# Layer 1's softmax numerators go to scratch memory, and the freed buffers keep K and V blocks

## The chip, the cores and the metric

One Trainium2 chip, one core. The metric is device time in microseconds from start to end of one launch. Each kernel is run several times, and the median is given.

## What is computed

Four layers in a row, with one token: attention, feed-forward, attention, feed-forward, and then the gradient of all of it. Both attention layers use the same cached K and V (4 heads of 65,536 keys, 128 wide, bfloat16; 67 MB each), and 32 query heads, 8 to each K/V head. Both feed-forward layers share their weights too.

```
x = x + A(layernorm(x))     # A: q = x@wq, softmax(q k^T / sqrt(128)) v, @wo
x = x + B(layernorm(x))     # B: relu(x@w1 + b1)^2 @ w2 + b2
x = x + A(layernorm(x))
x = x + B(layernorm(x))
out, vjp = jax.vjp(forward, ...); return (out, *vjp(grad_out))
```

The outputs are the result and the gradients of x, K, V, wq, wo, w1, b1, w2 and b2. The gradients of K and V are as large as K and V, and each is the sum over the two attention layers.

## The kernel before

K and V do not fit on the chip, so they are streamed four times. The passes are numbered 0 to 3. Pass 0 (`attn_fwd`, named L1) is the first attention layer forward, pass 1 (`attn_fwd`, L3) the second one forward, pass 2 (`attn_bwd3`) the second one's backward for the query gradient, and pass 3 (`attn_bwd4`) does the first one's backward together with the gradients of K and V for both layers, and writes them. Between passes lie the dense parts (wo, w1, w2, wq), with nothing of K and V to do.

**Blocks.** On-chip memory for streaming is one `ARENA`, cut into 20 blocks of 128 partitions x 4096 bfloat16, 1 MB each (1.0486e6 bytes). Everything large takes such a block: 32 keys x 128 partitions of K or of V (a head has 16 blocks), a piece of a weight, a tile of gradients waiting to be stored, or a numerator plane. `take_one` and `take_pair` hand out free blocks, oldest first as a rule, when the program is built; a load then waits on the chip until the last user of its block is done. `HELD` blocks are not handed out. Loads are issued by the SP queue in program order, and most are 2 MB (two neighbouring blocks). Stores are issued by the POOL queue.

**Numerator planes.** A pass over a head computes scores, and ACT writes exp(score - running maximum) as bfloat16 into the head's plane (`E`, one block for each layer and head). Pass 2 reads the planes of layer 3, pass 3 those of both layers. So 8 of the 20 blocks (`NSLOT` = 12 are left) end up held from the forward passes to pass 3, where `E_done` frees both planes of a head as it is finished.

**Kept blocks.** Consecutive passes run through the heads and keys in opposite directions, so the last blocks of one pass are the first of the next. `NKEEP = [8, 7, 7]` blocks stay on the chip between passes 0 and 1 (K), 1 and 2 (V), 2 and 3 (V), and are not loaded again. Kept K in pass 0 and kept V in pass 2 are stored transposed (`turned_to`). In pass 1, V is used untransposed, so kept V blocks are turned by an added transpose in `v8` (`early_turn`, L1117 in the profile), all but those of the last three loads of the pass.

**A step** is 1024 keys: 8 tiles of 128. In pass 0 and 1, stage `kT` transposes 8 K tiles on PE and copies them out of PSUM (L164 on DVE, L161 on ACT), `kS` makes the scores two steps later, and `v8` multiplies numerators and V 36 steps after `kT` (`FWD_LAG`). A head is 64 steps, a pass 256. In pass 2, `vT`, `vS` and `k8` do the same with V first. Passes 0 to 2 have their PE, DVE and ACT order as written; in pass 3 a scheduler orders the instructions.

**Pass 3** has for each block: `vT` and `vS` (dP by PE into the one score buffer `ps_dp`), DVE's product of dP and the numerators of both layers into `X` (L1370), POOL's copy of the numerators of both layers side by side into `xin` (L1330, one buffer), PE transposes of `xin` and `X` (L1336), gradient products on PE (L1393) whose results ACT and DVE convert into a block, and a 1 MB store from POOL (L1399). `k8` (L1424) is the query gradient. The V side runs up to 16 steps ahead of the rest at the start. The weight gradients are made in the background and stored from POOL too.

Of the kernel before, what the change touches and what calls it, by code (L numbers as in the profile page):

```python
# [10 lines left out]
BF = mybir.dt.bfloat16  # L11
# [5 lines left out]
P = 128  # L17
# [3 lines left out]
def kernel(  # L21
# [44 lines left out]
    TLEAD = 2  # L66
    STORE_STEPS = 5
    WAIT_STEPS = 5
    NSLOT = 12
    NWT = 6  # L70
    NKEEP = [8, 7, 7]
    NRING = 5

    const = ctx.enter_context(tc.tile_pool(name="const", bufs=1))
# [179 lines left out]

    BLK = J * DH
    JW = 2 * J
    NG = NSLOT + 2 * G
    assert C * R == BLK
    ARENA = slotp.tile([P, NG * BLK], BF, name="arena")
    GRAN = [ARENA[:, i * BLK:(i + 1) * BLK] for i in range(NG)]  # L260
# [4 lines left out]
    def wide(i):  # L265
        return ARENA[:, i * BLK:(i + 2) * BLK]

    def plane(lay, g):
        return NSLOT + G * lay + g

    def hold(i):
        HELD.add(i)
# [544 lines left out]
    def after(n, fn):  # L817
        TASKS.setdefault(NOW["i"] + n, []).append(fn)
# [52 lines left out]
        return L  # L871


    EALL = ARENA[:, NSLOT * BLK:].rearrange("p (l g c r) -> p l g c r", l=2, g=G, r=R)

    def E(lay, g, c0, n):
        assert plane(lay, g) in HELD and plane(lay, g) not in BUSY
        return EALL[:, lay, g, c0:c0 + n, :]

    def E2(g, c0, n):  # L880
        return EALL[:, :, g, c0:c0 + n, :].rearrange("p l c r -> p c l r")

    def E_done(g, c0, n):

# [5 lines left out]
    def split2(t):  # L890
        return t.rearrange("p c (l r) -> p c l r", l=2)


    def gsl(g):
        return slice(g * R, (g + 1) * R)
# [89 lines left out]
    def attn_fwd(p, L, on_group, bg, end=()):  # L985
# [56 lines left out]
        def stats(g, su, S, pm):  # L1042
            first = su == first_su[g]
            nm = L["negm"][:, g, su, :]
            v = {}

            def lows():
                pmn = tmp.tile([P, R], F32, name="pmn")
                if SU > HB:
                    pmx = tmp.tile([P, R], F32, name="pmx")  # L1050
                    nc.vector.tensor_reduce(out=pmx[:], in_=pm[:, :, :], axis=AX.X, op=ALU.max)
                    pin = pmx[:]
                else:
                    pin = pm[:, :, 0]
                if first:
                    nc.vector.tensor_scalar(out=pmn[:], in0=pin, scalar1=-SCALE, scalar2=None, op0=ALU.mult)
                else:
                    nc.vector.scalar_tensor_tensor(out=pmn[:], in0=pin, scalar=-SCALE, in1=L["negm"][:, g, prev_su[(g, su)], :],
                                                   op0=ALU.mult, op1=ALU.min)
                v["pmn"] = pmn  # L1060

            def turn():
                v["ptm"] = ps_mv([R, P], F32)
                nc.tensor.transpose(v["ptm"][:, :], v["pmn"][:, :], ident_f[:, :])

            def low():
                gm = tmp.tile([R, 1], F32, name="gm")
                nc.vector.tensor_reduce(out=gm[:], in_=v["ptm"][:], axis=AX.X, op=ALU.min)
                v["gmb"] = tmp.tile([R, P], F32, name="gmb", bufs=1)
                nc.vector.tensor_scalar(out=v["gmb"][:], in0=ones_f[0:R, :], scalar1=gm[:, 0:1], scalar2=None, op0=ALU.mult)  # L1070

            def spread():
                v["pnb"] = ps_mv([P, R], F32)
                nc.tensor.matmul(v["pnb"][:, :], lhsT=v["gmb"][:, :], rhs=ident_f[0:R, 0:R], start=True, stop=True)

            def exps():
                nc.vector.tensor_copy(out=nm, in_=v["pnb"][:])  # L1077
                if not first:
                    df = tmp.tile([P, R], F32, name="df")
                    nc.vector.tensor_tensor(out=df[:], in0=nm, in1=L["negm"][:, g, prev_su[(g, su)], :], op=ALU.subtract)  # L1080
                    al = spool.tile([P, R], F32, name="al", tag="al", bufs=3)
                    nc.scalar.activation(out=al[:], in_=df[:], func=ACTF.Exp)
                    state[("al", g, su)] = al
                v["rs"] = spool.tile([P, R], F32, name="rs", tag="rs", bufs=3)
                state[("rs", g, su)] = v["rs"]
                add_load(act=R * 0.5, dve=1.2)

            def exp2(h0):
                def f():
                    c0 = su * SU  # L1090
                    for h in (h0, h0 + 1):
                        nc.scalar.activation(out=E(p, g, c0, SU)[:, :, h], in_=S[:, h, :], func=ACTF.Exp,  # L1092
                                             bias=L["negm"][:, g, su, h:h + 1], scale=SCALE, accum_out=v["rs"][:, h:h + 1])
                return f
            for n, fn in ((1, lows), (3, turn), (4, low), (6, spread), (7, exps), (7, exp2(0)), (8, exp2(2)), (9, exp2(4)), (10, exp2(6))):
                after(n, fn)

        def v8(g, c8):
            su = c8 // SU
# [45 lines left out]
        def group_out(g, su, on):  # L1145
            nc.vector.reciprocal(out=L["rZ"][:, gsl(g)], in_=state["pz"][:])
            nc.vector.tensor_tensor(out=L["oT"][:, gsl(g)], in0=on[:], in1=L["rZ"][:, gsl(g)], op=ALU.mult)
            nc.vector.tensor_copy(out=L["oTb"][:, gsl(g)], in_=L["oT"][:, gsl(g)])
            on_group(g)
            fd = tmp.tile([P, NSU, R], F32, name="fd")  # L1150
            nc.vector.tensor_tensor(out=fd[:], in0=L["negm"][:, g, su, :].unsqueeze(1).to_broadcast([P, NSU, R]),
                                    in1=L["negm"][:, g, :, :], op=ALU.subtract)
            nc.scalar.activation(out=L["fw"][:, g, :, :], in_=fd[:], func=ACTF.Exp)
# [2 lines left out]
        early_turn = set(k for k in TOUCH[p][:-3] if k in KV["keep"])  # L1156
        n = len(items) // G
        order = list(dict.fromkeys(g for g, _ in items))
        holds = [(k * n + 2, plane(p, g)) for k, g in enumerate(order) if k > 0]
        if p == 0:  # L1160
            holds.append((len(items) - 40, plane(1, ITEMS[1][0][0])))
        with tc.manual_schedule(engines=ORDERED):
            pipeline(items, [(kT, 0), (kS, TLEAD), (v8, FWD_LAG)], bg, end, holds)
        st.close()
# [100 lines left out]
    def attn_bwd4(p, La, Lb, on_group, bg, stack, end=()):  # L1265
# [5 lines left out]
        state = {}  # L1271
        gfirst = {g: next(c8 for gg, c8 in items if gg == g) for g in range(G)}
        glast = {g: [c8 for gg, c8 in items if gg == g][-1] for g in range(G)}
        sufirst, sulast = {}, {}
        for g, c8 in items:
            sufirst.setdefault((g, c8 // SU), c8)
# [50 lines left out]
        def eIn(g, c8):  # L1327
            if c8 % J == 0:
                xin = dspool.tile([P, J, R2], BF, name="xin", tag="xin", bufs=1)
                nc.gpsimd.tensor_copy(out=split2(xin[:, :, :]), in_=E2(g, c8, J))  # L1330
                state["xin"] = xin

        def x_transpose(src):
            pt = ps_tr()
# [6 lines left out]
        def vS(g, c8):  # L1341
            if c8 == gfirst[g]:
                g_setup(g)
            vt = state.pop(("vt", g, c8))
            for i in range(8):
                s = (c8 + i) % J
                if s == 0:
                    state["ps_dp"] = ps_sc([P, J, R2])
                    nc.tensor.matmul(state["ps_dp"][:, :, :].rearrange("p c r -> p (c r)"), lhsT=sel2[:, :],
                                     rhs=state["ndt"][:, :].unsqueeze(1).to_broadcast([64, J, R2]), start=True, stop=False)  # L1350
                w = min(4, J - s)
                nc.tensor.matmul(state["ps_dp"][:, s:s + w, :].rearrange("p a b -> p (a b)"), lhsT=vt[:, i, :],  # L1352
                                 rhs=DOB[:, g, 0:w, :].rearrange("p a b -> p (a b)"), start=False, stop=(s == J - 1))
            if is_turned("v", g, c8):
                kv_done("v", g, c8)
                if c8 % J == J - 8 and nexts:
                    NOW["newest"] = True
                    kv8(*nexts.popleft())
                    NOW["newest"] = False
                    NOW["ring"] = not nexts  # L1360
            if (c8 + 8) % J == 0:
                c0 = c8 + 8 - J
                ps_dp = state["ps_dp"]
                if g == items[0][0]:
                    if c8 == J - 8 + items[0][1]:
                        state["Xs"] = Slot("xs")
                    X = state["Xs"].t.rearrange("p (n j r) -> p n j r", j=J, r=R2)[:, c0 // J % 8, :, :]
                else:
                    X = dspool.tile([P, J, R2], BF, name="X", tag="X", bufs=3)
                nc.vector.tensor_tensor(out=split2(X[:, :, :]), in0=split2(ps_dp[:, :, :]), in1=E2(g, c0, J), op=ALU.mult)  # L1370
                add_load(dve=0.13 + J * R2 * 0.00105)
                state[("X", g, c0 // J)] = X

# [59 lines left out]
                    on_group(g)  # L1433

        start_pass(p)
        for b in range(2):
            kv8("k", *items[b * J // 8])
        RING.update(sorted(FREE)[:2])
# [139 lines left out]
        yield from g_mv(w2_slabs()[0], FC, DC, lambda kc: L["gb"][:, kc:kc + 1], ps, fin, side=side)  # L1578


    hold(plane(0, ITEMS[0][0][0]))
    L1["n"], L1["nb"], L1["rstd"] = ln_fwd(x0, "L1")
    run(g_q(L1, 0, ps_mv))
    nc.vector.tensor_copy(out=x1[:], in_=x0[:])
# [290 lines left out]
```

## Time and profile before

| | |
|---|---|
| median of 3 runs | 1956.67 us (1956.1 to 1964.63) |
| the profiled execution: time | 1959.29 us |
| the profiled execution: span | 1957.5 us |
| PE, DVE, ACT, POOL busy | 82%, 60%, 53%, 7% |
| mean granted TensorE clock | 0.912 |
| moved by the transfers | 787.65 MB, mean 402 GB/s |

The span runs from the first to the last instruction of one execution. PE is the matrix engine, PEld its weight loads, DVE the vector engine, ACT the scalar engine, POOL GpSimd, SP the engine that issues loads. The slices cut the span into 40 equal parts of 48.9 us. Rows of groups read: line, engine, operation, tile written <- tile read, shapes, count, then busy time in us and the mean of one in ns, then the idle time before them and what ended it. PE's busy time overlaps weight loads and is not a measure of its peak. By the trace pass 0 runs to about 350 us, pass 1 from about 400 to 745, pass 2 from about 785 to 1140, pass 3 from about 1180 to the end.

### The profile page before, as it was taken

Reading aid. Unit: us, or ns where it says so; the run is one execution under the profiler, and the core shown is the slowest. Engines: PE = TensorE matmul, PEld = TensorE weight load, DVE = VectorE, ACT = ScalarE, POOL = GpSimd, SP = SyncE. Lnnn points to the kernel's source line nnn. Section 1 sums busy time; section 2 is a strip of 40 time slices with the busy share of each in tenths; the row PEclk is TensorE's granted clock in tenths of the full one; section 3 lists DMA queues with packets and bytes.
Section 4 is the critical chain, followed back from the end, with each engine's and each line's share of the span. In section 5 each row is a group of like instructions: output and inputs, shape, how many; then the busy total and the mean of one; then the engine's idle time right before and its main releaser. Section 6 shows DMA issues by size and latency. Waiting matters only on the chain. (4 is left out here: it accounts for less than half of the span.)

```text
span 1957.5 us, 67228 instructions
## 1 busy us (share of the span) xinstructions
PE 1609.0 (82%) x30319; PEld 1313.9 (67%) x30319; DVE 1169.7 (60%) x2421; ACT 1039.4 (53%) x1600; POOL 142.1 (7%) x321
## 2 busy tenths in 40 slices
PE   6878788687878878878787888887888898789897
PEld 6878778687877778777776885554555465455554
DVE  5655455255545544535454576766777686767666
ACT  3444334254334444436363455766777686667666
POOL 0000000000000000000000001111111111111211
PEclk9999999699999999999899998888897898788978
DMA  9999999999999999899999987999999999999996
GB/s 395 426 427 427 426 427 410 400 400 425 428 426 427 428 412 315 328 425 428 426 423 420 403 319 283 415 425 403 384 424 424 426 424 411 370 424 424 424 405 259
DMA packets 106015, 787.65 MB, mean 402 GB/s; under 512 B 9329, under 2 KB 16511, under 8 KB 42111
## 3 DMA queue, kind: packets, MB, share of 16 engines
q1 hardware_dynamic: 81646, 617.65, 76.7%
q0 software_dynamic: 24080, 165.70, 20.3%
q8 instruction: 237, 3.88, 0.7%
q14 instruction: 52, 0.42, 0.1%
HBM read 617.62 MB, written 165.69 MB: 400 GB/s over the span
## 5 line engine op out<-in xcount | busy, mean ns | idle before, releaser
L164 DVE COPY kt<-ps_tr 128x1024 bf16<-128x1024 bf16 x724 | 496.5, 688 | 423.8 <-PE ps_tr L1009 243.7
L161 ACT CAST arena<-ps_gg 128x1024 bf16<-128x1024 f32 x457 | 445.9, 1012 | 224.7 <-PE ps_gg L1393 140.7
L1009 PE MATMUL ps_tr<-ident_b,arena 128*128 128x128 bf16 x3840 | 307.9, 225 | 40.2 <-DMA arena<-in_A_k_cache_dram 29.7
L164 DVE CAST arena<-ps_gg 128x1024 bf16<-128x1024 f32 (+2 forms) x186 | 222.3, 1195 | 112.4 <-PE ps_gg L1471 46.9
L161 ACT COPY kt<-ps_tr 128x1024 bf16<-128x1024 bf16 x164 | 171.1, 1049 | 191.9 <-PE ps_tr L1201 114.9
L1009 PEld LDWEIGHTS <-arena 128*128 128x128 bf16 x3840 | 232.8, 101 | 48.9 <-DMA arena<-in_A_k_cache_dram 32.7
L1111 PE MATMUL ps_acc<-arena 128*128 128x64 bf16 (+4 forms) x4096 | 205.9, 196 | 59.8 <-DMA arena<-in_A_v_cache_dram 50.0
L1393 PE MATMUL ps_gg<-GG,xt 64*128 64x512 bf16 x1024 | 218.2, 423 | 27.3 <-DVE arena L164 10.8
L1111 PEld LDWEIGHTS <-arena 128*128 128x128 bf16 x4096 | 159.6, 100 | 65.8 <-DMA arena<-in_A_v_cache_dram 54.4
L1092 ACT ACTIVATE arena<-S_sb,L_negm 128x128 bf16<-128x128 f32 x256 | 165.6, 1003 | 58.4 <-DVE L_negm L1077 48.6
L1027 PE MATMUL ps_sc<-L_qpad,kt 128*128 128x64 bf16 (+7 forms) x3584 | 182.3, 194 | 15.6 <-ACT kt L161 7.4
L1201 PE MATMUL ps_tr<-ident_b,arena 128*128 128x128 bf16 x1920 | 155.3, 226 | 43.9 <-DMA arena<-in_A_v_cache_dram 40.5
L1321 PE MATMUL ps_tr<-ident_b,arena 128*128 128x128 bf16 x1824 | 181.9, 236 | 6.5 <-DMA arena<-in_A_v_cache_dram 3.8
L1027 PEld LDWEIGHTS <-kt 128*128 128x128 bf16 x3584 | 152.3, 100 | 19.4 <-ACT kt L161 9.8
L1321 PEld LDWEIGHTS <-arena 128*128 128x128 bf16 x1824 | 119.9, 105 | 63.6 <-issue 57.2
L1201 PEld LDWEIGHTS <-arena 128*128 128x128 bf16 x1920 | 117.5, 101 | 47.2 <-DMA arena<-in_A_v_cache_dram 42.1
L1424 PEld LDWEIGHTS <-arena 128*128 128x128 bf16 x2048 | 95.7, 103 | 60.3 <-issue 42.7
L1092 ACT ACTIVATION_READ_ACCUMULATOR arena<-S_sb,L_negm 128x1 f32 x256 | 127.9, 500 | 0.0
L1352 PEld LDWEIGHTS <-kt 128*128 128x128 bf16 x1824 | 85.1, 103 | 50.6 <-issue 49.2
L1352 PE MATMUL ps_sc<-DOB,kt 128*128 128x64 bf16 (+3 forms) x1824 | 115.0, 200 | 0.0
L1424 PE MATMUL ps_acc<-X,arena 128*128 128x64 bf16 (+3 forms) x1536 | 102.1, 200 | 12.5 <-DMA arena<-in_A_k_cache_dram 12.5
L1393 PEld LDWEIGHTS <-xt 64*128 64x128 bf16 x1024 | 64.3, 94 | 71.5 <-issue 34.1
(306 smaller groups left out, 2183.2 us busy)
## 6 DMA issues: line engine op xcount, KB each, us to landing
arena<-in_A_k_cache_dram SPq DMA_DIRECT2D x86, 2048.0 KB, 20.7
arena<-in_A_v_cache_dram SPq DMA_DIRECT2D x83, 2048.0 KB, 21.0
out_dram<-arena POOLq DMA_DIRECT2D x149, 1024.0 KB, 13.4
arena<-in_A_v_cache_dram SPq DMA_DIRECT2D x76, 1024.0 KB, 16.4
arena<-in_A_k_cache_dram SPq DMA_DIRECT2D x76, 1024.0 KB, 15.4
arena<-in_A_wo_dram SPq DMA_DIRECT2D x22, 1024.0 KB, 17.8
arena<-in_B_w_dram SPq DMA_DIRECT2D x21, 1024.0 KB, 8.7
arena<-in_A_wq_dram SPq DMA_DIRECT2D x20, 1024.0 KB, 14.7
```

The costliest lines, as they stand in the source:

```text
L161: nc.scalar.copy(out=out, in_=in_)
L164: nc.vector.tensor_copy(out=out, in_=in_)
L1009: nc.tensor.transpose(pt[:, i, :], kb8[:, i, :], ident_b[:, :])
L1027: nc.tensor.matmul(state["ps_s"][:, s:s + w, :].rearrange("p a b -> p (a b)"), lhsT=kt[:, i, :], rhs=L["qpad"][:, g, 0:w, :].rearrange("p ...
L1092: nc.scalar.activation(out=E(p, g, c0, SU)[:, :, h], in_=S[:, h, :], func=ACTF.Exp, bias=L["negm"][:, g, su, h:h + 1], scale=SCALE, accum_ ...
L1111: nc.tensor.matmul(ps_o[:, 0:w, :], lhsT=vb8[:, i, :], rhs=E(p, g, c, w), start=(c % SU == 0), stop=(c % SU == SU - 1), skip_group_check=True)
L1201: nc.tensor.transpose(pt[:, i, :], vb8[:, i, :], ident_b[:, :])
L1321: nc.tensor.transpose(pt[:, i, :], vb8[:, i, :], ident_b[:, :])
L1352: nc.tensor.matmul(state["ps_dp"][:, s:s + w, :].rearrange("p a b -> p (a b)"), lhsT=vt[:, i, :], rhs=DOB[:, g, 0:w, :].rearrange("p a b - ...
L1393: nc.tensor.matmul(pg[:, 512 * h:512 * h + 512], lhsT=xt[64 * h:64 * h + 64, j1 // 8 + m, :], rhs=gg[64 * h:64 * h + 64, :, :].rearrange(" ...
L1424: nc.tensor.matmul(ps_dq[:, 0:w, :].rearrange("p a b -> p (a b)"), lhsT=kb8[:, i, :], rhs=X[:, s:s + w, :].rearrange("p a b -> p (a b)"), ...
```

## The change

Layer 1's numerator planes no longer stay on the chip. In pass 0 only two blocks hold them, in turn, and each finished plane is stored to scratch memory in DRAM from POOL. In pass 3 each is loaded again by SP into a free block, 14 steps before its head begins (the first at the start of the pass). The last two heads' blocks are given back when the head is done. The arena has 20 blocks as before, with 4 of them for planes of layer 3 (`NSLOT` 16 and 4), and `NKEEP` becomes `[12, 11, 10]`. Since the two planes of a head no longer lie at a fixed distance, the copy into `xin` and the product into `X` are written as two instructions each, one for each layer.

```diff
-    NSLOT = 12
+    NSLOT = 16
-    NKEEP = [8, 7, 7]
+    NKEEP = [12, 11, 10]
...
-    NG = NSLOT + 2 * G
+    NG = NSLOT + G
...
+    FIRST2 = (NSLOT - 2, NSLOT - 1)
+    PLANE = {(1, g): NSLOT + g for g in range(G)}
...
     def plane(lay, g):
-        return NSLOT + G * lay + g
+        return PLANE[(lay, g)]
...
+    E_OUT = {g: edram.tile([P, BLK], BF, name="e_out%d" % g) for g in range(G)}
+
+    def e_store(g):
+        nc.gpsimd.dma_start(out=E_OUT[g][:, :], in_=GRAN[plane(0, g)])
+
+    def e_load(g):
+        sl = Slot("e_in", load=True)
+        PLANE[(0, g)] = sl.i
+        BUSY.discard(sl.i)
+        HELD.add(sl.i)
+        nc.sync.dma_start(out=GRAN[sl.i], in_=E_OUT[g][:, :])
...
# attn_fwd, stats
+            if p == 0 and su == last_su[g]:
+                after(11, lambda: e_store(g))
...
# attn_fwd, group_out
+            if p == 0 and g in order[-2:]:
+                HELD.discard(plane(0, g))
+                give_slot(plane(0, g), STORE_STEPS)
...
-        holds = [(k * n + 2, plane(p, g)) for k, g in enumerate(order) if k > 0]
         if p == 0:
-            holds.append((len(items) - 40, plane(1, ITEMS[1][0][0])))
+            holds = [(len(items) - 40, plane(1, ITEMS[1][0][0]))]
+        else:
+            holds = [(k * n + 2, plane(p, g)) for k, g in enumerate(order) if k > 0]
...
# attn_bwd4, eIn
-                nc.gpsimd.tensor_copy(out=split2(xin[:, :, :]), in_=E2(g, c8, J))
+                for lay in range(2):
+                    nc.gpsimd.tensor_copy(out=split2(xin[:, :, :])[:, :, lay, :], in_=E(lay, g, c8, J))
...
+            k = place[(g, c8)] + 14
+            if k % (len(items) // G) == 0 and k < len(items):
+                e_load(items[k][0])
...
# attn_bwd4, vS
-                nc.vector.tensor_tensor(out=split2(X[:, :, :]), in0=split2(ps_dp[:, :, :]), in1=E2(g, c0, J), op=ALU.mult)
+                for lay in range(2):
+                    nc.vector.tensor_tensor(out=split2(X[:, :, :])[:, :, lay, :], in0=split2(ps_dp[:, :, :])[:, :, lay, :],
+                                            in1=E(lay, g, c0, J), op=ALU.mult)
...
# attn_bwd4, before the first loads
         start_pass(p)
+        e_load(items[0][0])
...
# before pass 0
-    hold(plane(0, ITEMS[0][0][0]))
+    for k, g in enumerate(dict.fromkeys(g for g, _ in ITEMS[0])):
+        PLANE[(0, g)] = FIRST2[k % 2]
+    for i in FIRST2:
+        hold(i)
```

More of the change, by code (lines that the diff above doesn't have):

```diff
@@ L266, in wide @@
         return ARENA[:, i * BLK:(i + 2) * BLK]
+    FIRST2 = (NSLOT - 2, NSLOT - 1)
+    PLANE = {(1, g): NSLOT + g for g in range(G)}
+    KEPT_E = {}
     def plane(lay, g):
-        return NSLOT + G * lay + g
+        return PLANE[(lay, g)]
     def hold(i):
@@ L871, in new_layer @@
         return L
-    EALL = ARENA[:, NSLOT * BLK:].rearrange("p (l g c r) -> p l g c r", l=2, g=G, r=R)
+    EALL = ARENA[:, :].rearrange("p (b c r) -> p b c r", b=NG, r=R)
+    edram = ctx.enter_context(tc.tile_pool(name="edram", bufs=1, space=bass.MemoryType.DRAM))
+    E_OUT = {g: edram.tile([P, BLK], BF, name="e_out%d" % g) for g in range(G)}
[7 more added lines that the diff above has]
+        nc.sync.dma_start(out=GRAN[sl.i], in_=E_OUT[g][:, :])
     def E(lay, g, c0, n):
         assert plane(lay, g) in HELD and plane(lay, g) not in BUSY
-        return EALL[:, lay, g, c0:c0 + n, :]
-    def E2(g, c0, n):
-        return EALL[:, :, g, c0:c0 + n, :].rearrange("p l c r -> p c l r")
+        return EALL[:, plane(lay, g), c0:c0 + n, :]
     def E_done(g, c0, n):
@@ L1273, in attn_bwd4 @@
         glast = {g: [c8 for gg, c8 in items if gg == g][-1] for g in range(G)}
+        place = {it: k for k, it in enumerate(items)}
         sufirst, sulast = {}, {}
```

## The prediction

> **What bounds the kernel now.** I read the page first: the slices, then the bytes.
>
> ```profile
> span 1957.5 us, 67228 instructions
> ...
> DMA  9999999999999999899999987999999999999996
> GB/s 395 426 427 427 426 427 410 400 400 425 428 426 427 428 412 315 328 425 428 426 423 420 403 319 283 415 425 403 384 424 424 426 424 411 370 424 424 424 405 259
> ...
> HBM read 617.62 MB, written 165.69 MB: 400 GB/s over the span
> ```
>
> Transfers fill nearly every slice, at about 427 GB/s where only K and V are read (passes 0 to 2) and about 424 where gradients are also written (pass 3). Slices 15, 16, 23 and 24 are the dense parts between passes, the last is the end. So a megabyte taken out of a pass shortens it, if the engines can follow. Next, the windows by stage (columns: busy PE, PEld, DVE, ACT, POOL, granted clock, DMA share, GB/s):
>
> ```profile
> 300.00:420.00 120.00, 90.71 (x2138) 86.38 (x2135) 52.37 (x148) 41.02 (x83) 0.61 (x13) 0.83 0.98 398
> 420.00:690.00 270.00, 219.37 (x5223) 208.79 (x5219) 147.02 (x335) 117.21 (x284) 0.00 (x0) 0.96 1.01 427
> 690.00:830.00 140.00, 117.77 (x2744) 112.21 (x2742) 67.99 (x179) 66.46 (x114) 0.00 (x0) 0.95 0.91 347
> 830.00:1100.00 270.00, 213.84 (x4821) 198.53 (x4819) 132.43 (x254) 121.39 (x164) 0.00 (x0) 0.94 1.01 424
> 1100.00:1240.00 140.00, 119.90 (x2330) 98.09 (x2330) 94.15 (x208) 77.81 (x90) 13.20 (x35) 0.95 0.88 328
> 1240.00:1560.00 320.00, 268.08 (x3297) 168.84 (x3290) 226.95 (x410) 220.28 (x260) 54.88 (x106) 0.87 1.00 415
> 1560.00:1890.00 330.00, 284.91 (x3538) 177.25 (x3537) 235.85 (x415) 225.05 (x267) 58.63 (x109) 0.86 1.00 413
> ```
>
> In the passes PE is busy about 80%, in pass 3 84 to 86%. That is close enough that added PE work can matter, not so close that it sets the pace. Third, what the queue that issues the loads waits for (us in total, times, longest):
>
> ```profile
> SPq L352 <- PE ps_acc L1424: 345.2, 45, 21.9
> SPq L357 <- PE ps_tr L1009: 264.2, 60, 19.5
> SPq L357 <- PE ps_acc L1111: 185.0, 34, 11.6
> SPq L352 <- PE ps_tr L1321: 138.3, 36, 25.4
> ```
>
> It waits for a block to come free, while the transfer engines still have work queued. More blocks help only where those engines run dry: 690 to 830, 1100 to 1240, and small dips in pass 3.
>
> One block is 1.0486 MB: 2.46 us at 427 GB/s, 2.47 us at 424. All terms below are against the profiled execution (span 1957.5, own time 1959.3); the median shown, 1956.67, is 2.6 us under that time, and I take the same difference from it.
>
> **Pass 0: four stores added.** Each group's numerators are one block, issued from POOL, whose queue has nothing else between start and pass 1's end. Read-only slices are full, so each store takes its 2.46 us from the loads: 4 x 2.46 = +9.8. The last store falls at about 300 to 420 us, where 398 of 427 GB/s leaves 120 x 29/427 = 8.1 us of transfer time unused; I count half of it: **+8.6** (7.4 to 9.8). Near the end of pass 0 the kept K leave 5 or 6 free blocks where 7 were. A 1 MB V load there took 14.8 us from issue to landing (median up to 400 us); five in flight are 12.3 us of work, still ahead of PE. I add **+0.5** (0 to 2.5, one block's time). Group 2's exponentials on ACT write over group 0's block and so wait for its store, issued some 100 steps, over 100 us, before: no cost.
>
> The row for issuing a 1 MB store from POOL in pass 3 is 532 ns at the median and 596 ns at most, beside DVE at 71%. The Trainium skill (SBUF — State Buffer, SBUF: two separate sides) speaks against such stores: a POOL-issued transfer cannot write its descriptors while VectorE holds the shared ports. By that rule each of the four could wait out a copy; the 596 ns maximum shows none, and the first reader of the data is three passes away.
>
> **Pass 1: four K blocks fewer.** 4 x 2.46 = **-9.8**. These blocks are also already transposed, so 128 transposes and 16 evacuations leave PE, DVE and ACT. Cover: the first 48 steps (32 before) need no K load, V is needed only from step 36, and loads fill whatever PE frees. If PE were the limit there the gain would be lost; at 80% busy it is not.
>
> **Pass 2: four V blocks fewer.** Again **-9.8**. But four more V blocks are turned in pass 1's tail (`early_turn` goes from 4 to 8 blocks): 16 x 8 transposes. In the tail the groups and the timeline say:
>
> ```profile
> L1117 PE MATMUL ps_tr<-ident_b,arena 128*128 128x128 bf16 x128 | 9.9, 219 | 2.2 <-ACT arena L161 2.2
> ...
> L161 ACT COPY arena<-ps_tr 128x1024 bf16<-128x1024 bf16 x8 | 8.9, 1128 | 3.5 <-PE ps_tr L1117 3.5
> ```
> ```profile
> 745.52 1.06 PE L1111 MATMUL ps_acc<-arena 128*128 128x64 bf16 x32 [1.51 <-DMA arena<-in_A_v_cache_dram]
> ```
>
> The present 128 took from 726.8 to 742 with their V products, 0.95 us a step, against 0.61 us for a V load's quarter. The same number again could cost up to 16 x 0.34 = 5.4. Yet the tail ends with PE waiting 1.51 us for the last V, so some of it is hidden, and pass 2's start, where PE and not the transfers is late, gets the 128 transposes back. I take **+2** (-2 to +5.4).
>
> **Pass 3: three V blocks fewer, four numerator loads more.** One block net, **+2.5**. The first load is queued on SP ahead of the first K load, which went out at 1171.4; loads there landed after 6 to 8 us, so numerators arrive near 1179; the K loads behind it on SP are first used in step 27. The first POOL copy was at 1176.2, its transposes at 1185.0, the first X product at 1187.1: no cost (0 to 6). Later ones are queued 14 steps, over 35 us, ahead.
>
> POOL's `xin` copy and DVE's X product are each cut in two:
>
> ```profile
> L1330 POOL COPY xin<-arena x64: 609/614/673, 1176.1 to 1909.9; 128x512 bf16<-128x512 bf16 x64
> ```
> ```profile
> L1370 DVE TENSOR_TENSOR X<-ps_sc,arena x48: 669/680/692, 1356.0 to 1927.0; 128x512 bf16<-128x512 f32 x48
> ```
>
> A 128x128 DVE cast from PSUM took 283 ns, so 256 elements by the line through both points are 416, two halves 0.83: +0.15 x 64 = 9.7 us of DVE. For POOL, 128x128 casts took 370 and 128x512 614, so two halves are about 0.90: +0.29 x 64 = 18 us. Neither is on the path (DVE 71%, POOL 17%); only the single score buffer waits for X, 9.6 us over the whole pass. **+1** (0 to 10).
>
> **Slots.** Pass 2 runs in 16 blocks instead of 12, pass 3's groups in 15, 16, 17, 18 instead of 12, 14, 16, 18. Below 424 GB/s pass 3 loses 320 x 9/424 = 6.8 us in its first stretch and 330 x 11/424 = 8.6 us in the second. Three more blocks are 7.4 us of lead, more than the longest single dip (2.9 us, 1380 to 1390), if PE, which falls behind there at a granted clock of 0.64, can catch up afterwards. I take two thirds of the first, a tenth of the second, and 0.6 of pass 2's 1.9: **-6** (0 to -12). The holes at 690 to 830 and 1100 to 1240 stay: 5 or 6 blocks beside the kept ones, as now.
>
> Sum: 8.6 + 0.5 - 9.8 - 9.8 + 2 + 2.5 + 1 - 6 = -11.0, so 1956.67 - 11.0 = **1945.7**.
>
> By bytes alone the change is 11 blocks out, 8 in: -3 blocks, -7.4 us at 427 GB/s. The Trainium skill (DMA: Bandwidth & Descriptors, Where 436 GB/s comes from) gives 358 GB/s as a core's share of memory with the neighbour busy; by it the same bytes would be -8.8 us, an estimate, but the 427 row decides.
>
> **Rivals.**
> *Bytes only.* The extra blocks recover nothing because the dips follow the PE clock (0.64 at 1380, 0.50 at 1670), and the turning costs its 5.4: -11 + 6 + 3.4 = -1.6, 1955.1. For it: PE is 99% busy in the dips at 1380 and 1630. Against: PE is idle right before, 0.98 of the 10 us from 1360.
>
> *POOL's order, the slow side.* In the built program, eight of the 64 blocks have ten store issues, in POOL's order, between the halves of `xin`. Such an issue waited for staged results 291.2 us in 79 times, 3.7 each, longest 18.2. Behind it stand the second half, then PE's transposes, then the gradient products and the stores. Two steps of about 3 us (777 us over 256) cover it; it decides once a wait passes 6 us. Ten issues at the 9.6 us seen within 1400 to 1660 are 10 x (9.6 + 0.5 - 6) = +41; half of that gives 1945.7 + 20 = 1966. Against: PE waited only 0.7 us for `xin` in the whole pass.
>
> *More than counted.* The stores hide and slots return all they can: -11 - 1 - 6 = 1938.5.
>
> *Not done as said.* The built program loads 244 K and 235 V blocks instead of 248 and 242, with four stores and four loads of numerators; excluded.
>
> **Chances.** Forecast 0.55, bytes only 0.20, POOL's order 0.17, more than counted 0.08. 0.5% (9.8 us) is about what a measurement of this kernel can tell from no change. The forecast's own range is 1939 to 1952; a fifth of it lies within 0.5%. Faster 0.44 + 0.08 = 0.52, same 0.11 + 0.20 = 0.31, slower 0.17. The range 1934 to 1962 leaves out most of POOL's order and a little below.
>
> **What would show it.** Right: 7.3 MB less read and 4.2 MB more written, pass 0 about 9 us longer, passes 1 and 2 each about 9 shorter, pass 3's first half above 415 GB/s. Wrong: pass 0 unchanged or over 12 longer, PE waiting on `xin` or on X at 1185, GB/s below 420 in passes 1 and 2, or pass 3 longer by more than 3.

## The result and the profile after

The changed kernel takes 1970.53 us (median of 6 runs, 1965.99 to 1975.09), the kernel before 1957.14 in the same comparison: ratio 1.0054 [1.0035, 1.0074], slower by 7 to 14 us. The forecast was 1945.7 in a range of 1934 to 1962. The profiled execution took 1972.71 us, with a span of 1970.9.

The page of the kernel after, with the rows that answer to the first fence of before:

```profile
span 1970.9 us, 66875 instructions
...
DMA  9999999899999997699999988999999999999995
GB/s 394 426 427 425 429 428 392 337 356 424 428 425 428 428 425 263 247 426 428 425 429 420 421 326 312 421 414 394 423 418 423 425 413 423 403 423 424 424 400 220
...
HBM read 610.28 MB, written 169.88 MB: 396 GB/s over the span
```

The bytes are as forecast: 7.3 MB less read, 4.2 MB more written. But the rate fell, from 400 to 396 GB/s, and it fell in certain places: counted from 0, slices 7 and 8 (the end of pass 0 and the dense part behind it) were 400 and 400 before and are 337 and 356 now, slices 15 and 16 (the end of pass 1 and the dense part behind it) were 315 and 328 and are 263 and 247.

By stages, cut at the same instructions in both timelines (the last sum of the softmax denominator, L212, ends a forward pass; its first score products begin one), in us:

| | before | after | difference | forecast |
|---|---|---|---|---|
| pass 0 | 368.5 | 387.3 | +18.8 | +9.1 |
| dense part | 44.6 | 47.9 | +3.3 | 0 |
| pass 1 | 334.1 | 334.0 | -0.1 | -7.8 with the turning |
| dense part | 44.8 | 47.1 | +2.3 | 0 |
| pass 2 and the dense part behind it | 393.5 | 385.7 | -7.8 | -9.8 and what the slots give |
| pass 3 | 772.0 | 768.9 | -3.1 | +3.5 and what the slots give |

Two stages hold most of the error: pass 0 lost twice what was counted, and pass 1 gained nothing. The row of the dense part between passes 1 and 2 in the kernel before, for later comparison:

```profile
747.18:792.00 44.82, 39.16 (x876) 37.70 (x876) 22.60 (x75) 15.55 (x17) 0.00 (x0) 0.96 0.78 266
```

**The end of pass 0.** What the queue of loads issues there (start, us that the run of issues lasted, queue and line, transfer, count):

```profile
334.84 2.16 SPq L356 DMA_DIRECT2D arena<-in_A_v_cache_dram  x3
347.98 0.33 SPq L361 DMA_DIRECT2D arena<-in_A_v_cache_dram  x1
348.42 16.23 SPq L356 DMA_DIRECT2D arena<-in_A_v_cache_dram  x3
367.13 1.31 SPq L453 DMA_DIRECT2D arena<-in_A_wo_dram  x2
369.00 1.23 SPq L356 DMA_DIRECT2D arena<-in_A_v_cache_dram  x2
```

and PE's timeline of the same stretch (the bracket is the idle time before, and what ended it):

```profile
357.95 0.61 PE L1127 MATMUL ps_acc<-arena 128*128 128x64 bf16 x8 [9.12 <-DMA arena<-in_A_v_cache_dram]
...
382.58 1.89 PE L1127 MATMUL ps_acc<-arena 128*128 128x64 bf16 x32 [8.31 <-DMA arena<-in_A_v_cache_dram]
```

L361 is the load of two neighbouring blocks, L356 that of one. After 337.0 nothing is issued for 11 us, until a pair is free at 347.98; the next three single loads take 16 us because each waits for a block. PE then waits twice for V, 9.12 and 8.31 us, where its longest such wait before was 5.58.

**The end of pass 1.** The last 20 us of the pass in 10-us windows (busy PE, PEld, DVE, ACT, POOL with counts, clock, DMA share, GB/s), the groups of the turned blocks from 690 to 790 us, and the same groups of turn4, a run told below that turns four of these blocks fewer:

```profile
749.20:759.20 10.00, 7.00 (x156) 6.72 (x153) 3.77 (x8) 8.91 (x22) 0.00 (x0) 1.00 0.86 322
759.20:769.20 10.00, 8.00 (x212) 7.67 (x209) 3.56 (x11) 4.38 (x5) 0.00 (x0) 1.00 0.62 207
```
```profile
L1133 PE MATMUL ps_tr<-ident_b,arena 128*128 128x128 bf16 x256 | 19.5, 219 | 3.0 <-ACT arena L161 3.0
...
L161 ACT COPY arena<-ps_tr 128x1024 bf16<-128x1024 bf16 x16 | 17.6, 1112 | 8.2 <-PE ps_tr L1133 8.2
...
L164 DVE COPY arena<-ps_tr 128x1024 bf16<-128x1024 bf16 x16 | 11.0, 690 | 14.4 <-PE ps_tr L1133 14.0 <-DMA arena<-in_A_v_cache_dram 0.4
```
```profile
L1133 PE MATMUL ps_tr<-ident_b,arena 128*128 128x128 bf16 x128 | 9.9, 219 | 2.2 <-ACT arena L161 2.2
L161 ACT COPY arena<-ps_tr 128x1024 bf16<-128x1024 bf16 x8 | 8.9, 1130 | 3.2 <-PE ps_tr L1133 3.2
```

The transfers fall off: the last V block has been issued at 744.75, 24.5 us before the end of the pass. In the kernel before that distance was 15.8 us. Of ACT's 8.91 us in the first window only 4.97 are copies of turned blocks, the rest is exponentials. ACT and DVE share the copies, and both wait for PE's transposes (8.2 and 14.0 us) more than PE waits for ACT (3.0 us). The extra turning stands behind the last load, where no load of V covers it.

### The profile page after: what moved, and what is told of

Same layout as the page of the kernel before. It is cut to its first block, busy times and chain, and to the rows that moved or that the text cites. A ratio compares the mean times of both kernels' runs of the same rounds, so it can differ in the third digit from the quotient of the medians.

```text
span 1970.9 us, 66875 instructions
## 1 busy us (share of the span) xinstructions
PE 1599.0 (81%) x30095; PEld 1306.7 (66%) x30095; DVE 1160.4 (59%) x2461; ACT 1036.2 (53%) x1596; POOL 157.4 (8%) x389
## 5 line engine op out<-in xcount | busy, mean ns | idle before, releaser
L164 DVE COPY kt<-ps_tr 128x1024 bf16<-128x1024 bf16 x668 | 457.8, 688 | 408.3 <-PE ps_tr L1023 232.5
L161 ACT CAST arena<-ps_gg 128x1024 bf16<-128x1024 f32 (+1 forms) x449 | 439.4, 1012 | 209.4 <-PE ps_gg L1420 112.8
L1023 PE MATMUL ps_tr<-ident_b,arena 128*128 128x128 bf16 x3712 | 299.1, 226 | 36.9 <-DMA arena<-in_A_k_cache_dram 24.7
L1023 PEld LDWEIGHTS <-arena 128*128 128x128 bf16 x3712 | 226.1, 101 | 45.8 <-DMA arena<-in_A_k_cache_dram 27.1
L161 ACT COPY kt<-ps_tr 128x1024 bf16<-128x1024 bf16 x148 | 154.3, 1047 | 191.8 <-PE ps_tr L1221 111.4
L1127 PEld LDWEIGHTS <-arena 128*128 128x128 bf16 x4096 | 160.5, 101 | 81.4 <-DMA arena<-in_A_v_cache_dram 64.5
L1342 PE MATMUL ps_tr<-ident_b,arena 128*128 128x128 bf16 x1728 | 173.9, 236 | 12.1 <-DVE kt L164 10.5
L1041 PE MATMUL ps_sc<-L_qpad,kt 128*128 128x64 bf16 (+7 forms) x3328 | 170.1, 194 | 13.8 <-issue 7.6
L1221 PE MATMUL ps_tr<-ident_b,arena 128*128 128x128 bf16 x1792 | 144.8, 226 | 40.9 <-DMA arena<-in_A_v_cache_dram 38.7
L1041 PEld LDWEIGHTS <-kt 128*128 128x128 bf16 x3328 | 141.8, 100 | 17.8 <-issue 8.9
L1342 PEld LDWEIGHTS <-arena 128*128 128x128 bf16 x1728 | 113.3, 105 | 59.3 <-issue 55.2
L1221 PEld LDWEIGHTS <-arena 128*128 128x128 bf16 x1792 | 109.5, 101 | 45.0 <-DMA arena<-in_A_v_cache_dram 41.4
L1451 PEld LDWEIGHTS <-arena 128*128 128x128 bf16 x2048 | 94.3, 104 | 48.4 <-issue 36.4
L578 ACT ACTIVATE mv_t<-mv_t 128x1024 bf16<-128x1024 bf16 x96 | 101.9, 1063 | 20.6 <-DVE mv_t L589 20.5
L1266 PE MATMUL ps_acc<-dsT,arena 128*128 128x64 bf16 (+7 forms) x2048 | 102.2, 194 | 12.5 <-DMA arena<-in_A_k_cache_dram 9.4
L1377 PE MATMUL ps_sc<-DOB,kt 128*128 128x64 bf16 x1728 | 112.3, 201 | 0.0
## 6 DMA issues: line engine op xcount, KB each, us to landing
arena<-in_B_w_dram SPq DMA_DIRECT2D x21, 1024.0 KB, 10.4
```

The costliest lines, as they stand in the source:

```text
L161: nc.scalar.copy(out=out, in_=in_)
L164: nc.vector.tensor_copy(out=out, in_=in_)
L578: nc.scalar.activation(out=t[:, :], in_=t[:, :], func=ACTF.Copy, accum_out=y[:, kc:kc + 1])
L1023: nc.tensor.transpose(pt[:, i, :], kb8[:, i, :], ident_b[:, :])
L1041: nc.tensor.matmul(state["ps_s"][:, s:s + w, :].rearrange("p a b -> p (a b)"), lhsT=kt[:, i, :], rhs=L["qpad"][:, g, 0:w, :].rearrange("p ...
L1127: nc.tensor.matmul(ps_o[:, 0:w, :], lhsT=vb8[:, i, :], rhs=E(p, g, c, w), start=(c % SU == 0), stop=(c % SU == SU - 1), skip_group_check=True)
```

## The experiments

Theory first held (A): the 12 kept blocks of K leave too few free blocks for V at the end of pass 0. Rivals: that the stores cost more than their bytes (B); that loads of two neighbouring blocks are what waits, since the lists of blocks to be loaded singly (`KV["halves"]`) are those of the kernel before with its 8 kept blocks (C). Ratios are to the kernel before, run on the same chip in the same comparison.

**Ten blocks of K kept instead of twelve** (keep10).

```diff
-    NKEEP = [12, 11, 10]
+    NKEEP = [10, 11, 10]
```

> The changed kernel with NKEEP = [10, 11, 10], so two more blocks are free at the end of pass 0 and two more K blocks are loaded in pass 1. Theory A (too few free blocks in pass 0's tail: V loads wait for a block and PE for V, which cost about 9 us of pass 0's +18.8 and 3 us of the dense part): pass 0 ends near 378 us instead of 387, the dense part after it is back near 45, pass 1 gets at most 4.9 longer; total 1960 to 1966. Theory B (the four stores cost twice their bytes): pass 0 still ends near 387, total about 1975. Theory C (loads of two blocks wait for neighbouring free blocks): in between, 1965 to 1970.

Measured: 1955.64 us, 0.9982 [0.9966, 0.9999]. Pass 0 fell to 378.7, the dense part behind it to 45.3, pass 1 was 333.2. So two kept blocks fewer give back 8.6 and 2.6 us in the stages that A names. The median is even lower than A expected; 4.9 us of it lie from the end of pass 1 to pass 3 (427.9 against 432.8), where as many blocks are kept in both. Single profiles of that stage differ by as much (see the stores alone).

**As many blocks kept as before** (keep8_7_7): the stores, the loads of numerators and the free blocks of the change, with none of them used to keep more.

```diff
-    NKEEP = [12, 11, 10]
+    NKEEP = [8, 7, 7]
```

> The changed kernel with the old NKEEP = [8, 7, 7]: planes still go to scratch memory and back, and the freed blocks only stream. By bytes it costs 4 stores and 4 loads, 8 x 2.46 = 19.7 us, against the kernel before, less what more free blocks return. Theory A: pass 0 ends 9 to 10 us after the one before (378), pass 1 and 2 as long as before, pass 3 up to 10 longer; total 1968 to 1977. Theory B: pass 0 ends near 387, total 1980 to 1987. If free blocks return much, total below 1966.

Measured: 1958.05 us, 0.9991 [0.9979, 1.0004], the last case of the expectation. Pass 0 is 378.3, pass 1 331.7, and from the end of pass 1 to pass 3 it takes 432.6 us where the kernel before took 438.3. This was the surprise of the study: 19.7 us of stores and loads of numerators were added, nothing was saved, and the time is that of the kernel before.

**Single loads over a longer stretch** (halves).

```diff
-        KV["halves"] = set(TOUCH[p][-8:] + (TOUCH[p][:10] if p else []))
+        KV["halves"] = set(TOUCH[p][-20:] + (TOUCH[p][:18] if p else []))
```

> The changed kernel with more loads of one block instead of two: the last 20 blocks of every pass and the first 18 of passes 1 to 3, instead of 8 and 10. Theory C: SP no longer stands at a two-block load in pass 0's tail (334.8 to 348.0) and at pass 1's start (to 434.8); pass 0 shorter by 4 to 8 us, the hole at 430 to 440 (205 GB/s) gone, total 1958 to 1965. Theory A: the number of blocks is what counts, single loads return at most 3 us, total 1967 to 1971. Theory B: no change, 1970.

Measured: 1954.59 us, 0.9973 [0.9961, 0.9986], with all 12, 11 and 10 blocks kept, below all that C expected. Pass 0 is 378.35, pass 1 326.8. So A in its plain form falls: twelve kept blocks do not starve pass 0 by themselves; it is twelve kept blocks and a load that must wait for two neighbouring free ones (C). Whether it matters that the two are neighbours, or only that there must be two, no run separates. For the dense part behind pass 0 it is the other way round: it still takes 48.0 us here and 45.3 in keep10, so there the number of free blocks counts.

**The stores alone**, put into the kernel before (before_stores).

```diff
...
+    E_OUT = {g: edram.tile([P, BLK], BF, name="e_out%d" % g) for g in range(G)}
+
+    def e_store(g):
+        nc.gpsimd.dma_start(out=E_OUT[g][:, :], in_=GRAN[plane(0, g)])
...
+            if p == 0 and su == last_su[g]:
+                after(11, lambda: e_store(g))
```

> The kernel before with the four stores of pass 0 alone added; nothing reads them back, planes stay where they are, NKEEP is the old one. Theories A and C: each store costs its bytes, 4 x 2.46 less up to one that hides: pass 0 ends at 376 to 378 instead of 368.5, total 1964 to 1967. Theory B: pass 0 ends near 387, total 1975. If the stores hide, total 1957.

Measured: 1973.03 us (median of 4), 1.0076 [1.0054, 1.0097], or 11 to 19 us. Pass 0 is 378.3 (+9.8, the bytes exactly) and pass 1 unchanged, so in pass 0 the stores cost about what A and C said and not twice that (B). The total is above what A and C expected all the same. In the profile, of the fastest of the four executions (1968.90), another 3.9 us lie between pass 1's end and pass 3 (442.2 against 438.3), where the program is the same. Why is open. So a difference of 4 us in that stage, from one profile each, says little.

Next, which end the single loads mend: the end of the passes (halves_tail) or their start (halves_start), and whether they would have helped without the change (before_halves).

```diff
# halves_tail
+        KV["halves"] = set(TOUCH[p][-20:] + (TOUCH[p][:10] if p else []))
# halves_start
+        KV["halves"] = set(TOUCH[p][-8:] + (TOUCH[p][:18] if p else []))
# before_halves: the kernel before
+        KV["halves"] = set(TOUCH[p][-20:] + (TOUCH[p][:18] if p else []))
```

> The changed kernel with the last 20 blocks of each pass loaded singly (8 in the change), the start of each pass as in the change. Theory T (with 12 blocks of K kept, the last V loads of pass 0 must wait for two neighbouring free blocks; the start of pass 1 is a second, separate loss): pass 0 back from 387.3 to about 378.3, pass 1 still about 334, so 1959 to 1964. Rival S (single loads are simply better everywhere, ends and starts alike, half of the 16 us each way whatever is kept): 1959 to 1965 as well, but then pass 2's end gains too. Rival N (the 16 us came mostly from the start of pass 1): 1966 to 1971.

Measured: 1959.03 us, 0.999 [0.9977, 1.0004]. Pass 0 378.8, as T said; pass 1 330.5, 3.5 less than T said (its end is loaded singly too). The dense part between them is not mended; pass 0 and that part, first of the kernel after, then of this run:

```profile
0.00:387.30 387.30, 289.73 (x6669) 277.75 (x6669) 192.99 (x460) 149.41 (x355) 4.17 (x41) 0.91 0.98 407
387.30:435.24 47.94, 36.10 (x810) 34.51 (x811) 22.68 (x65) 14.82 (x17) 0.61 (x13) 0.75 0.92 361
```
```profile
0.00:378.80 378.80, 289.25 (x6670) 276.08 (x6670) 192.88 (x460) 149.51 (x355) 4.19 (x41) 0.91 1.00 418
378.80:427.10 48.30, 36.55 (x810) 34.92 (x811) 22.60 (x65) 14.89 (x17) 0.61 (x13) 0.72 0.92 355
```

> The changed kernel with the first 18 touched blocks of passes 1 to 3 allowed to load singly (10 in the change), the ends as in the change. Theory T: pass 0 stays at about 387, pass 1 shortens from 334.0 to about 327 to 329, so 1961 to 1966. Rival N (most of the gain is the start): 1955 to 1960. If neither end alone recovers anything, above 1968.

Measured: 1962.22 us, 1.0011 [0.9996, 1.0027]. Pass 0 386.35, so not mended; pass 1 328.5. Pass 1 now begins with 12 kept blocks, so the first ten blocks that it touches, the only ones of its start that the change allows to be loaded singly, are all on the chip already. Its first real loads are pairs, and its first 10 us move less than the 427 GB/s of halves. The same window of the kernel before, of the kernel after and of halves:

```profile
413.10:423.10 10.00, 8.68 (x243) 8.51 (x243) 2.43 (x7) 3.02 (x6) 0.00 (x0) 0.84 0.83 324
```
```profile
435.20:445.20 10.00, 8.64 (x241) 8.46 (x241) 2.44 (x7) 2.97 (x6) 0.00 (x0) 0.84 0.95 375
```
```profile
426.30:436.30 10.00, 8.67 (x244) 8.49 (x244) 2.44 (x7) 3.11 (x6) 0.00 (x0) 0.84 1.02 427
```

The kernel before was slower still there (324), so this loss is not new; with 8 kept and four more free blocks (keep8_7_7) it is gone, 437 GB/s in that window.

> The kernel before with the same wider sets of single loads (last 20, first 18). Theory T (pairs only hurt where 10 to 12 blocks are kept): within 4 us of the kernel before, 1954 to 1961. Rival S (single loads help any kernel at the ends of passes): 8 to 16 us less, 1941 to 1951; then the change itself would cost about as much as it seemed to.

Measured: 1956.1 us, 0.9976 [0.9964, 0.9988]: about 5 us less, inside theory T's window by the median and just outside its 4 us by the ratio. Against 16 us for the changed kernel (1.0054 to 0.9973), most of the loss belongs to the change, some 5 us of it were there before.

Next, the V side. Keeping 11 and 10 blocks of V with 8 of K (keep8_11_10), and all the change with only the four turned blocks of before (turn4):

```diff
# keep8_11_10
-    NKEEP = [12, 11, 10]
+    NKEEP = [8, 11, 10]
# turn4
-        early_turn = set(k for k in TOUCH[p][:-3] if k in KV["keep"])
+        early_turn = set(k for k in TOUCH[p][:-3] if k in KV["keep"] and k[2] < 7)
```

> The changed kernel with 8 blocks of K kept (as before) and 11 and 10 of V. Beside the run with 8, 7 and 7 kept it prices the V side alone, beside the changed kernel the K side. Theory F (a block that is kept and a free block that is filled while the dense part runs are worth the same; the gap between passes 1 and 2 moved 315 GB/s with 7 kept, 225 with 11): dense part and pass 2 together within 4 us of the 432.6 us with 7 kept, pass 0 about 378, so 1954 to 1960, no better than with 8, 7 and 7. The forecast's sum (four V blocks are -9.8, one of pass 3 saved again, turning +2): 1946 to 1951.

Measured: 1964.93 us, 1.003 [1.0017, 1.0043]. Slower than with 7 and 7 kept, outside every expectation. Pass 1 takes 339.8 us against 331.7 (+8.1), and from there to pass 3 it is 432.7 against 432.6: four blocks of V, 9.8 us of loads, no longer read, and nothing gained. (The profile is of the slowest of its 12 executions, 1971.29 us, which lost 4.6 us more in pass 3; the medians differ by 0.0039, 7.6 us.) The windows of the dense part between passes 1 and 2 say why; the kernel after, keep8_11_10, and keep8_7_7:

```profile
769.22:816.30 47.08, 40.61 (x876) 38.84 (x877) 22.61 (x75) 15.65 (x17) 0.00 (x0) 0.92 0.68 225
```
```profile
762.10:808.30 46.20, 40.55 (x876) 38.75 (x877) 22.63 (x75) 15.55 (x17) 0.00 (x0) 0.91 0.68 229
```
```profile
754.45:802.93 48.48, 41.28 (x875) 39.55 (x876) 22.64 (x75) 15.75 (x17) 0.00 (x0) 0.93 0.83 315
```

48.48 us at 315 GB/s are 15.3 MB, 46.2 at 229 are 10.6: 4.7 MB, 4.5 blocks, more. With four blocks free instead of kept, four more are read in advance while the engines do the dense part and the transfers stand half idle. Within what a profile tells of this stage, a kept block and a free block buy the same there, and the free one needs no turning.

> The changed kernel, but only 4 of the kept V blocks are turned at the end of pass 1, as before; the other kept ones are turned in pass 2. The forecast's +2 (-2 to +5.4) for turning: pass 1 two to five us shorter, pass 2 a little longer, 1965 to 1970. If turning is hidden: within 2 us of the changed kernel, 1968 to 1973. If turned blocks are what pass 2 gained by: 1973 to 1978.

Measured: 1960.58 us, 1.001 [1.0, 1.002], below all three expectations. Pass 1 is 325.8 us against 334.0 (-8.2), and from there to pass 3 430.2 against 432.8, so pass 2 does not pay for it. Its last 20 us of pass 1, beside the two windows of the kernel after above:

```profile
737.90:747.90 10.00, 7.81 (x169) 7.35 (x166) 4.17 (x10) 8.02 (x19) 0.00 (x0) 1.00 1.00 391
747.90:757.90 10.00, 7.75 (x215) 7.48 (x212) 2.96 (x10) 4.85 (x8) 0.00 (x0) 1.00 0.84 299
```

The transfers hold longer (391 and 299 GB/s instead of 322 and 207), and the last V issue is 16.4 us before the end instead of 24.5.

The kernel after, keep8_11_10, turn4 and keep8_7_7 make a square, and its sides agree in pass 1: four more blocks of V turned cost +8.1 (with 8 of K, and four more of V kept for it) and +8.2 (with 12, and as many kept); four more of K kept save 5.8 (with 8 turned) and 5.9 (with 4).

Last, candidates to beat both kernels: single loads with 10, 11 and 10 kept, the same with 8, 7 and 7, and the first with four turned blocks.

> The changed kernel with 10 instead of 12 blocks of K kept and the wider sets of single loads: candidate to beat both. If the two edits mend different stages (theory T: keep10 the end of pass 0 and the weights between passes, single loads the start of pass 1): 1946 to 1952. If they mend the same thing: 1953 to 1957, no better than either. If the forecast's sum holds once the starving is gone: 1945.

Measured: 1953.92 us, 0.9961 [0.9946, 0.9976], the second case: the two edits mend the same thing, and together they do no better, beyond the intervals, than either alone (0.9982 and 0.9973).

> The changed kernel with 8, 7 and 7 blocks kept as before and the wider sets of single loads: stores, loads of numerators and free blocks, but nothing more kept. Theory F (free blocks are worth as much as kept ones): within 4 us of the run with 10, 11 and 10 kept and single loads (1953.9), so 1951 to 1958. If keeping is worth its bytes (8 to 10 blocks, 20 us or more of transfer time): 1965 or above. If the narrow sets only hurt where blocks are short: equal to the run with 8, 7 and 7 (1958).

Measured: 1958.24 us, 0.9982 [0.9967, 0.9998], equal to keep8_7_7 (1958.05) as in the third case. Against keep10_halves, keeping more is worth 0.002, some 4 us, and the two intervals overlap: far from the 20 us of its bytes.

> The kernel with 10, 11 and 10 kept and wider single loads, with only 4 V blocks turned at the end of pass 1. Forecast's term of turning, +2 (-2 to +5.4): 1949 to 1953. Hidden: 1952 to 1956. Turning ahead is worth more than it costs (pass 2's start, where PE is late, gets 128 transposes back): 1956 to 1960.

Measured: 1953.63 us, 0.9969 [0.9957, 0.9981], the same as with eight turned, so the turning is hidden here. In its profile pass 1 is 4.4 us shorter, and from there to pass 3 takes 430.6 us against 425.2. By these profiles pass 2 pays the turning back; in the changed kernel it did not. Why the two differ is open: 425.2 is the lowest of all profiles of that stage, taken at a granted clock of 0.96 in pass 2 where turn4 and keep10_halves_turn4 had 0.94 and 0.93.

The best is keep10_halves, about 8 us below the kernel before. The one-line edit of the kernel before (0.9976) does most of that without the change, and the intervals of the two overlap.

## Why the prediction was wrong

**"Pass 0: four stores added", +8.6.** Right: +9.8 in pass 0 of before_stores, the upper end of the range. (Its total rose by 15 us; the rest is not explained.) The Trainium skill (SBUF — State Buffer, SBUF: two separate sides) says that a transfer issued from POOL cannot write its descriptors while a VectorE operation holds the ports that the two share. In this trace the four issues took 532 to 692 ns and landed after 10.4 to 13.1 us, and no instruction waited for them; a wait of a whole copy on each is not seen.

**"Near the end of pass 0 the kept K leave 5 or 6 free blocks where 7 were ... I add +0.5 (0 to 2.5)."** This failed, and it is the largest single miss. It measured +9.0 (387.3 against 378.3), and +3.3 more in the dense part, which the sum had at nothing. The step counted free blocks as if each served a load, but some loads there need two neighbouring ones, and the queue is in order, so what stands behind a waiting pair waits too (the 11 us from 337.0). The profile of before showed that pairs wait: the queue's second and third largest waits are those of the pair load, L357. With single loads (halves_tail) or two fewer kept (keep10) pass 0 is within 0.5 us of its bytes. The +3.3 is another thing: single loads leave it (48.0 and 48.3 us), fewer kept blocks remove most of it. Over the profiles of the changed kernel and its variants this part took 46.0 to 48.3 us with twelve blocks of K kept and 44.4 to 45.4 with eight or ten, so it goes with the number of free blocks.

**"Pass 1 ... -9.8. Cover: the first 48 steps need no K load ... and loads fill whatever PE frees."** Half right: four blocks of K are worth -5.8 and -5.9 in the pass. The rest goes with loads that were issued late: the dense part ahead moved 47.94 us at 361 GB/s (17.3 MB) against 18.4 MB in keep8_7_7 (44.44 us at 415), so 2.6 us of transfer time, and the first 10 us of pass 1 another 1.2 at 375 instead of 427 GB/s. The words "loads fill whatever PE frees" were true of the middle of the pass, and false of its start. With the single loads of halves the forecast's size comes back: dense part and pass 1 take 374.8 us against 384.2 in keep8_11_10, -9.4, while with 8 kept the single loads gain nothing there (376.9 against 376.2).

**Turning, "+2 (-2 to +5.4)".** This step failed too. It measured +8.1 and +8.2, outside the range. I took only the excess of a step over a load (0.34 us) sixteen times, as if the added work lay beside loads, and let pass 2 give some back. It lay behind the last load, so all of it counted. PE carried most of it; pass 1 of the kernel after and of turn4:

```profile
435.24:769.22 333.98, 268.91 (x6458) 256.91 (x6457) 170.95 (x397) 154.39 (x359) 0.00 (x0) 0.96 0.99 414
```
```profile
432.10:757.90 325.80, 262.39 (x6329) 249.81 (x6328) 165.84 (x389) 146.03 (x351) 0.00 (x0) 0.96 1.00 420
```

PE is busy 6.5 us longer (6.6 between keep8_7_7 and keep8_11_10), and it waits 0.8 us longer for ACT's copies of turned blocks. ACT's added copies take 8.4 us, about the whole cost, but ACT mostly waited for PE there; which of the two would have to be relieved, no run tests. The size holds with the old sets of single loads: with 10 blocks of K kept and the wider sets, eight turned or four gave the same total (0.9961 and 0.9969).

**"Pass 2 ... Again -9.8", and "the holes at 690 to 830 and 1100 to 1240 stay".** The profile of the changed kernel shows -5.5 from the end of pass 1 to pass 3, half of what was forecast there. But single profiles of that stage spread: seven with 11 and 10 blocks kept and eight turned took 425.2 to 432.8 us (mean 430.0), three with the old blocks 438.1 to 442.2 (mean 439.5). By the means it is -9.5, so that the size was wrong is not shown. What failed is the comparison behind it. keep8_7_7 and keep8_7_7_halves save none of V's loads and took 432.6 and 431.0, so four free blocks do nearly as much by themselves. Before the change the hole behind pass 1 ran at 266 GB/s, and with the same 7 blocks kept and four more free ones at 315 (keep8_7_7), so what it lacked was blocks to read into. The forecast counted the free blocks at 0.6 of 1.9 us here, let the hole stay as it was, and counted the kept ones in full.

**Pass 3, +2.5 and +1, and the slots -6.** The parts named for the slots (4.5, 0.9 and 1.1, the last for pass 2) add up to -6.5, not -6, and leave -1.9 for pass 3. The profile shows -3.1, but one execution of pass 3 does not hold that: over all profiles it took 767.3 to 772.0 us (mean 769.8) in the three kernels with the old pass 3, and 765.5 to 774.8 (mean 770.0) in the eleven with the new. No gain is shown, nor a loss. The first half ran at 404 GB/s (1202 to 1540; 398 in the same length before), not above 415. The cut operations were sized well and stand in the groups of the kernel after:

```profile
L1396 DVE TENSOR_TENSOR X<-ps_sc,arena 128x256 bf16<-128x256 f32 x96 | 36.4, 414 | 2.0 <-PE ps_sc L1377 1.5
...
L1361 PE MATMUL ps_tr<-ident_b,xin 128*128 128x128 bf16 x256 | 31.2, 234 | 1.1 <-POOL xin L1352 0.9 <-DVE xt L164 0.2
```

**The rivals.** POOL's order, the slow side, gave 1966, near what came. That is luck, for it is not what happened: PE waited 0.9 us for `xin` in all of pass 3, as in the row above. None of the four cases had the ends of the passes in it, where the time went. Of the signs of being wrong, the one of pass 0 ("over 12 longer") showed, at +18.8. Three numbers there are slightly off without bearing on the result: *more than counted* adds up to 1938.7; the window from 1670 to 1680 us (286 GB/s) is a deeper dip than the one called longest; and 0.98 us is PE's busy time, not its idle time, in the 10 us from 1360.

The terms as measured, in the profiled executions, each a difference between two runs (they add up because the runs form a chain: before, keep8_7_7, turn4, after): stores +9.8, tail of pass 0 +9.0, dense part +3.3, K kept -5.9, free blocks in pass 1 -2.4 (keep8_7_7 against before), turning +8.2, end of pass 1 to pass 3 -5.5, pass 3 -3.1: +13.4, which is 1970.9 - 1957.5.

## What to carry to other kernels

Before counting a kept block at the time of its load, ask what a free block would do in the same place: ahead of a stretch where the transfers stand half idle, it is filled there and saved nearly as much here. Keeping more moves the shortage to the ends of passes, where the queue is in order and a load that needs two neighbouring blocks holds up all behind it, so lists that were set for the old number have to move with it. And work that is put behind the last load of a pass has no load to lie beside: price it in full from those last windows, not by the average of the pass.

## What was not expected

Four stores and four loads of 1 MB, 19.7 us of transfer time, came out even once four more blocks were free, with no load saved (keep8_7_7, 0.9991 [0.9979, 1.0004]). And pass 3 is nearly blind to all of it: with 7 or 10 blocks kept, with its groups in more blocks or fewer, and with DVE's and POOL's operations cut in two, its mean stays at 770 us, with single profiles between 765.5 and 774.8. What sets it these runs do not tell.
